# The first three attention tiles in a new order, loads and weight conversions of the start regrouped

## Chip, core and metric

The kernel runs on one core of a Trainium2 chip. The metric is the time of one execution on the device, in microseconds; less is better. TensorE is PE, VectorE DVE, ScalarE ACT, GpSimd POOL, and SyncE (SP) issues most DMAs.

## What is computed

Block attention with a window and block means, a dense block with a gate, and a mixture of eight experts to which tokens are assigned greedily:

```python
scores_l = scale * q @ k^T, kept where |i - j| < 16
scores_s = scale * q @ max over 32 keys(k) + log(32)
a = softmax([scores_l, scores_s])
x = a @ [v, mean over 32 keys(v)]            # 2 batches, 8 heads, 768 x 64
h = x @ w_in                                 # x: 1536 x 512, w_in: 512 x 2048
x = (h * clip(h + 3, 0, 6) / 6) @ w_out
logits = x @ w_gate; each token to one expert, at most 192 tokens an expert
out = relu(x[mask] @ w1[e]) @ w2[e]          # 8 experts, 512 x 1024 and 1024 x 512
```

The weights come to the chip with 64 bits per number, and the kernel makes 32-bit numbers of them.

## The kernel before, in words

The 1536 tokens are 12 tiles of 128 (`NT`), and 4 units of 3 tiles (`UT`, `U` = 384 tokens, `NU` = 4). A tile's attention is done in two halves of four heads. A half (n, h) goes through these steps:

- scores on PE (`front`, L383) into banks 0 and 1, from the queries and from `kw`, the window of keys; DVE adds the mask and takes the minimum (L391, one instruction and a read for each of four pieces);
- exponentials on ACT (`soften`, L402, four pieces), then on DVE two small instructions on the sums (L404, L405; `sm` has two buffers), then one pass of POOL over `A` (L406, "scaling" below);
- transposition on PE (`turn`, L414) and its copy `at` on ACT (L416; two buffers);
- products with the values on PE (`values`, L429) from `VW`, which holds a window of values and the means of all blocks of 32 values; then `emit_x` (from L437): a copy `x` on ACT (L447) and its low half on DVE (L78).

`window` (L368) copies the window of keys for a tile on DVE. `q_prep` (L353, L355) transposes the queries of a tile from the fourth on. The means of the values are a sum on PE in bank 4 (`vsum_mul`, L199, eight products); `vsum_place` copies them on ACT into the three `VW` buffers (L204, three instructions one behind the other).

A slice of `w_in` (16 in all, f0 to f15 below) is loaded by SP into one of four buffers (`w_in_load`, L247), converted by three steps on DVE through bank 3 (L272, "steps" below), then split by `w_split` into `wh` on ACT (L289) and `wl` on POOL (L290). When a slice's third step has been written down, the load of the slice four places on is put on a list (`soon`), which is emitted behind the next piece of work. `gemm1` takes 12 products of PE (L621 to L623) for a slice and unit; ACT adds 3 and takes relu (L624), and DVE's `gate` (L637) sets free the bank, 5 or 6, that the product two slices later needs.

The instructions of each engine run in the order in which the program writes them down. `drive` interleaves several generators by the share of each that is done. Ahead of the first unit, `prologue` (halves of tiles 0 to 2) is interleaved with the first `4 * AHEAD` pieces of `splits` (conversion steps, with a split `CLAG` slices behind). In the first unit `gemm1` is interleaved with the attention of tiles 3 to 5 and the rest of `splits`; `ATTS`, `END`, `S0` and `S1` set how. Somewhere in the first unit SP also issues the loads of the second batch: four for the rows of its keys (L169), two for the sums of its values (L173), and `load_v` (L181) for windows of values. `warm` puts products on PE whose result nobody reads.

Of the kernel before, what the change touches and what calls it, by code (L numbers as in the profile page):

```python
# [42 lines left out]
STEPS = 12  # L43
SEEK, COUNT = 4600, 1900
ROUTE = 100000
CLAG = 2
AHEAD = 6
EARLY = 13
LEFT = 4
VLAG = 0  # L50
VN = 3
ATTS = [31212, 20565, 23910, 18810]
END = [0.92, 0.92, 0.92]
S0 = 0.27
S1 = 0.7
LX = 4
TAIL = [0, 1], [2]

# [30 lines left out]
def build(ctx, tc, q, k, v, w_in, w_out, w_gate, w1, w2, out):  # L89
# [82 lines left out]
    def load_first(x, src, b, hs, rs, r):  # L172
        SP.dma_start(x[:, hs, rs], src[b, hs].rearrange("h (p r) d -> p h r d", r=r)[:x.shape[0], :, rs])  # L173
# [11 lines left out]
    def vsum_load(b, g):  # L185
        load_first(vs, v, b, slice(0, H), RH[g], KR)
# [11 lines left out]
            means.append(bank(4))  # L198
        PE.matmul(means[-1][:KEYS], zones, vs[:, :, i], start=i == 0, stop=last)  # L199

    def vsum_place():
        pv = means[-1][WIN:KEYS, None].rearrange("p a (h d) -> p a h d", d=D).to_broadcast([NB, 2, H, D])
        for x in VW:
            ACT.activation(x[WIN:KEYS], pv, AF.Copy)  # L204

    for g in range(2):
        hs = slice(HP * g, HP * g + HP)
        for rs in RH:
            load_first(k0, k, 0, hs, rs, KR)
        load_first(q0, q, 0, hs, slice(0, UT), UT)  # L210

    for x in VW:
        POOL.memset(x, 0.0)
# [88 lines left out]
    def kprep_first(g):  # L302
        hps = slice(2 * g, 2 * g + 2)
        for i, rs in enumerate(RH):
            for hp in range(2 * g, 2 * g + 2):
                p = bank((2, 3, 5, 6)[2 * i + hp % 2])
                for j in range(4):
                    for z in range(2):
                        PE.matmul(p[64 * z:64 * z + 64, j * KP:(j + 1) * KP], k0[:, 2 * hp + z, 4 * i + j], ident[:KP, :KP],  # L309
                                  start=True, stop=True, skip_group_check=True)  # L310
                ACT.activation(kT[:, hp, rs], p[:, :4 * KP].rearrange("p (r s) -> p r s", r=4), AF.Copy)
                DVE.tensor_reduce((ks if i else kmax)[:, hp], p[:, :4 * KP].rearrange("p (r n s) -> p n r s", r=4, s=4),
                                  axis=AX.XY, op=OP.max)
                yield 450
        DVE.tensor_tensor(ks[:, hps], ks[:, hps], kmax[:, hps], op=OP.max)
# [57 lines left out]
    def front(n, h, after):  # L373
        b, i = divmod(n, 6)
        qT = fr[n] if n else qT0
        A = Abuf[(2 * n + h) % (LAG + 1)]
        sp = [bank(0), bank(1)]
        for pr in range(2):
            hp = 2 * h + pr
            for g in range(2):  # L380
                for s in range(2):
                    r, c = slice(64 * s, 64 * s + 64), slice(QG * g, QG * g + QG)
                    PE.matmul(sp[s][c, pr * KEYS:(pr + 1) * KEYS], qT[r, hp, c], kw[r, hp, g], start=True, stop=True)  # L383
        if after:
            q_prep(n + 1)
        mk = mask[:, 0 if i == 0 else 2 if i == 5 else 1]
        sm = att.tile([128, 3, 4], FT, name="sm", bufs=2)
        for pr in range(2):
            for s in range(2):
                c = 2 * pr + s  # L390
                DVE.tensor_tensor_reduce(out=A[:, c], in0=sp[s][:, pr * KEYS:(pr + 1) * KEYS], in1=mk, scale=-SCALE,  # L391
                                         scalar=3e38, op0=OP.add, op1=OP.min, accum_out=sm[:, 0, c:c + 1])
        if after:
            window(n + 1)
        later.append((A, sm))
# [11 lines left out]

    ats = {}

    def turn(n, h):  # L410
        A = Abuf[(2 * n + h) % (LAG + 1)]
        p = bank(2)
        for c in range(4):
            PE.transpose(p[:KEYS, c * 128:(c + 1) * 128], A[:, c], ident)  # L414
        at = att.tile([128, 4, 128], FT, name="at", bufs=2)
        ACT.activation(at[:KEYS], p[:KEYS].rearrange("p (c s) -> p c s", c=4), AF.Copy)  # L416
        ats[n, h] = at

# [34 lines left out]
    def halves():  # L453
        for n in range(UT, NT):
            b, i = divmod(n, 6)
            if b and i == 0:
                vsum(b)
                yield from kprep(b)
                q_prep(n)
                window(n)  # L460
                yield 2400
            for h in range(2):
                t = pend.pop(0) if len(pend) >= LAG else None
                if t:
                    turn(*t)
                    turned.append(t)
                    yield 660
                after = h == 1 and i < 5
                first = (n, h) == (UT, 1)
                if not first:  # L470
                    front(n, h, after)
                    yield 1250 + 450 * after
                pend.append((n, h))
                while turned:
                    if turned[0] == (6 * b, 0):
                        vsum_mul(0, True)
                        vsum_place()
                    values(*turned.pop(0))
                    yield 1000
                emit_x()  # L480
                if first:
                    yield 1
                    front(n, h, after)
                    yield 1250 + 450 * after
                yield from soften()
                emit_x()
                if (n, h) == (5, 0):
                    for j in range(4):
                        load_rows("kraw", k, 1, j)
                    for g in range(2):  # L490
                        vsum_load(1, g)
            if i == 5:
                while pend or turned:
                    if turned:
                        yield 700
                        values(*turned.pop(0))
                        yield 1000
                        emit_x()
                    if pend:
                        yield 800  # L500
                        t = pend.pop(0)
                        turn(*t)
                        turned.append(t)
                        yield 660
# [269 lines left out]
    def prologue():  # L774
        soft = []

        def half(n, h, after=False):
            front(n, h, after)
            soft.append(soften())
            next(soft[-1])  # L780
            pend.append((n, h))

        def rest():
            for _ in soft.pop(0):
                pass

        def turned_one():
            t = pend.pop(0)
            turn(*t)
            turned.append(t)  # L790

        for c in kprep_first(0):
            yield c
        qprep_first(0)
        window(0, slice(0, 2))
        yield 600
        for c in kprep_first(1):
            yield c
        front(0, 0, False)
        qprep_first(1)  # L800
        warm(6)
        soft.append(soften())
        next(soft[-1])
        pend.append((0, 0))
        yield 1850
        window(0, slice(2, 4))
        half(0, 1, True)
        warm(10)
        rest()
        yield 1250  # L810

        def block_means(i):
            for j in range(i, i + 2):
                vsum_mul(j, j == KR - 1)

        def both(t):
            values(*t)
            emit_x()

        half(1, 0)  # L820
        warm(6)
        rest()
        yield 1250
        turned_one()
        yield 660
        half(1, 1, True)
        warm(6)
        rest()
        yield 1700
        block_means(0)  # L830
        yield 1700
        turned_one()
        yield 660
        block_means(2)
        yield 1700
        half(2, 0)
        rest()
        yield 1250
        block_means(4)
        block_means(6)  # L840
        vsum_place()
        yield 3400
        warm(8)
        both(turned.pop(0))
        yield 1000
        turned_one()
        yield 660
        both(turned.pop(0))
        yield 1000
        half(2, 1, True)  # L850
        rest()
        yield 1700
        both(turned.pop(0))
        yield 1000
        turned_one()
        yield 660
        rest()
        yield from attend_unit(0)

    w_in_load(0)  # L860
    for g in range(2):
        vsum_load(0, g)
    load_v(0)
    w_in_load(1)
    w_in_load(2)
    load_v(1)
    w_in_load(3)
    load_rows("qraw", q, 0, UT)
    load_v(2)
    load_rows("qraw", q, 0, UT + 1)  # L870

    def splits():
# [6 lines left out]
            yield 1  # L879

    splitting, second = splits(), gemm2()
    drive([[prologue(), ATTS[0], 0, 1], [part(splitting, 4 * AHEAD), 4 * AHEAD, S0, 1.0]], soon)
    tlast = late = None
    for u in range(NU):
        st = []
# [427 lines left out]
```

## Time and profile before

| | |
|---|---|
| median of 3 runs | 579.42 us (577.53 to 581.66) |
| the profiled execution | 577.43 us |
| its span on the core | 575.3 us |
| mean granted clock of PE, share of full speed | 0.994 |
| PE busy | 551.1 us (96%) |
| DVE busy | 355.1 us (62%) |
| ACT busy | 295.2 us (51%) |
| POOL busy | 164.9 us (29%) |

The span begins with the first recorded work on the core and ends with the last; the 2.1 us between span and execution lie around it. All starts below count from the span's start. A busy PE does not mean a PE at full rate: the durations of neighbouring products overlap, so the space between the starts of two products is their price. In a row, a bracket behind an instruction gives the idle time of its engine ahead of it and what ended it.

### The profile page before, as it was taken

What the parts mean: (1) busy time and instruction counts of PE and PEld (TensorE: products, weight loads), DVE (VectorE), ACT (ScalarE), POOL (GpSimd) and SP (SyncE); (2) the same over time, 40 slices, a digit from 0 to 9 for tenths busy, and PEclk for the clock granted to TensorE, in tenths of its full rate; (3) what the DMA queues carried; (4) which work ended last, traced back from release to release, by engine and by line L of the source; (5) the groups of instructions that cost most, each with busy time, mean ns of one, the idle gap of its engine ahead of it and who ended that gap; (6) DMA issues with size and microseconds to landing.
All of it is one profiled execution on the core that took longest, in us unless ns stands there. A gap on an engine that the chain in (4) does not pass through costs nothing.

```text
span 575.3 us, 10978 instructions
## 1 busy us (share of the span) xinstructions
PE 551.1 (96%) x3939; PEld 463.2 (81%) x3939; DVE 355.1 (62%) x1020; ACT 295.2 (51%) x702; POOL 164.9 (29%) x198
## 2 busy tenths in 40 slices
PE   6979999999999999999999999999999999999993
PEld 6757889878899989976677777777889988998882
DVE  7778893634543497730055555644687888888870
ACT  4666664556555355651232232325576767676750
POOL 2235467011211033562244444455001110111011
PEclk9999999999999999999999999999999999999998
DMA  9998696122100254420070000014698978998811
GB/s 242 245 224 203 156 228 118 38 47 47 26 2 2 75 183 147 146 66 1 1 206 14 1 1 1 0 51 167 180 273 256 271 228 256 284 265 241 258 33 32
DMA packets 98270, 75.05 MB, mean 130 GB/s; under 512 B 38112, under 2 KB 84704, under 8 KB 98208
## 3 DMA queue, kind: packets, MB, share of 16 engines
q1 hardware_dynamic: 96224, 67.96, 44.0%
q0 software_dynamic: 1984, 6.32, 3.0%
q8 instruction: 33, 0.54, 0.4%
q14 instruction: 29, 0.24, 0.1%
HBM read 67.55 MB, written 6.71 MB: 129 GB/s over the span
## 4 chain that ended last, share of the span: by engine, by line
PE 57%; issue 26%; DVE 5%; POOL 4%; ACT 3%; DMA 3%; SPq 0%; POOLq 0%; DVEq 0%
PE bank L738 8%; PE bank L739 7%; PE bank L740 7%; PE bank L621 7%; PE bank L622 6%; PE bank L623 6%; POOL out_dram L1116 3%; PE bank L383 2%; PE bank L649 2%; PE bank L429 2%; PE bank L199 1%; DMA big<-in_moe_w_out_dram 1%; PE bank L414 1%; PE bank L309 1%; PE bank L573 1%
## 5 line engine op out<-in xcount | busy, mean ns | idle before, releaser
L621 PE MATMUL bank<-x,wh 128*128 128x384 f32 x256 | 91.5, 357 | 2.4 <-DVE t L637 2.2
L299 DVE TENSOR_TENSOR wl<-t,wh 128x1024 fp32r<-128x1024 f32 x64 | 77.0, 1220 | 20.5 <-ACT wh L298 19.9
L622 PE MATMUL bank<-x,wh 128*128 128x384 f32 x256 | 86.0, 336 | 0.4 <-DVE x L78 0.3
L623 PE MATMUL bank<-x,wl 128*128 128x384 f32 x256 | 86.1, 336 | 0.0
L715 ACT ACTIVATE thx<-t 128x384 fp32r<-128x384 f32 (+2 forms) x80 | 36.2, 459 | 94.6 <-PE bank L739 93.7
L624 ACT ACTIVATE t<-bank,three 128x384 f32<-128x384 f32 x64 | 37.1, 580 | 84.8 <-PE bank L623 83.3
L738 PE MATMUL bank<-wh,thx 128*128 128x512 f32 x192 | 79.2, 412 | 0.0
L716 POOL TENSOR_TENSOR tlx<-t,thx 128x384 fp32r<-128x384 f32 (+1 forms) x56 | 56.0, 1002 | 77.1 <-ACT thx L715 70.4
L740 PE MATMUL bank<-wh,tlx 128*128 128x512 f32 x192 | 75.3, 392 | 0.1
L739 PE MATMUL bank<-wl,thx 128*128 128x512 f32 x192 | 75.0, 390 | 0.0
L1141 PE MATMUL bank<-x,wh 128*128 128x384 f32 x256 | 73.7, 360 | 0.5 <-DVE x L1067 0.5
L298 ACT ACTIVATE wh<-t 128x1024 fp32r<-128x1024 f32 x64 | 65.6, 1047 | 0.0
L1143 PE MATMUL bank<-x,wl 128*128 128x192 f32 x256 | 64.2, 251 | 0.0
L637 DVE SCALAR_TENSOR_TENSOR t<-t,bank 128x384 f32<-128x384 f32 x64 | 34.9, 549 | 44.7 <-ACT t L624 44.7
L406 POOL TENSOR_TENSOR A<-A,sm 128x480 f32<-128x480 f32 x24 | 23.7, 987 | 113.5 <-ACT at L416 68.3
L1116 POOL DMA_INDIRECT out_dram<-t,idx x16 | 14.9, 930 | 141.5 <-DVE t L1165 136.0
L621 PEld LDWEIGHTS bank<-x,wh 128*128 128x128 f32 x256 | 48.0, 188 | 6.5 <-DVE t L637 3.6
L1143 PEld LDWEIGHTS bank<-x,wl 128*128 128x128 f32 x256 | 48.9, 191 | 0.3
L1141 PEld LDWEIGHTS bank<-x,wh 128*128 128x128 f32 x256 | 48.1, 188 | 1.2 <-DVE x L1067 0.8
L622 PEld LDWEIGHTS bank<-x,wh 128*128 128x128 f32 x256 | 48.2, 188 | 1.0 <-DVE x L78 0.9
L1157 PE MATMUL bank<-wh,t 128*128 128x512 f32 x128 | 49.0, 391 | 0.0
L623 PEld LDWEIGHTS bank<-x,wl 128*128 128x128 f32 x256 | 48.1, 188 | 0.0
(195 smaller groups left out, 1028.0 us busy)
## 6 DMA issues: line engine op xcount, KB each, us to landing
t<-in_moe_w_dram SPq DMA_DIRECT2D x128, 256.0 KB, 4.6
t<-in_moe_w_in_dram SPq DMA_DIRECT2D x16, 512.0 KB, 5.3
big<-in_moe_w_out_dram SPq DMA_DIRECT2D x16, 512.0 KB, 3.4
VW<-in_v_dram SPq DMA_DIRECT2D x20, 192.0 KB, 4.7
t<-in_v_dram SPq DMA_DIRECT2D x4, 768.0 KB, 12.2
raw<-in_q_dram SPq DMA_DIRECT2D x9, 256.0 KB, 4.1
t<-xs SPq DMA_DIRECT2D x8, 258.0 KB, 3.4
t<-in_k_dram SPq DMA_DIRECT2D x4, 384.0 KB, 5.6
```

The lines of the kernel that those rows point to most:

```text
L298: ACT.activation(hi, x, AF.Copy)
L299: DVE.tensor_tensor(lo, x, hi.bitcast(FT), op=OP.subtract)
L621: PE.matmul(p, wh[:, kk, :], xh[:, kk, :], start=kk == 0, stop=False)
L622: PE.matmul(p, wh[:, kk, :], xl[:, kk, :], start=False, stop=False)
L623: PE.matmul(p, wl[:, kk, :], xh[:, kk, :], start=False, stop=kk == KD - 1)
L716: (DVE if placed[0] else POOL).tensor_tensor(ths[i][1], t, ths[i][0].bitcast(FT), op=OP.subtract)
L738: PE.matmul(acc[j], th[:, c], WH[s], start=f == 0, stop=False)
L739: PE.matmul(acc[j], th[:, c], WL[s], start=False, stop=False)
L740: PE.matmul(acc[j], tl[:, c], WH[s], start=False, stop=f == NF - 1)
L1141: PE.matmul(p, a[:, kk, :], xt[:, kk].rearrange("p c s -> p (c s)"), start=kk == 0, stop=False, skip_group_check=True)
L1143: PE.matmul(p[:, :CAP], b[:, kk, :], xt[:, kk, 0, :], start=False, stop=kk == KD - 1, skip_group_check=True)
L1157: PE.matmul(p, x, w, start=m == 0 and i == 0, stop=m == NM - 1 and i == 2)
```

## The change

Four things are rewritten, all at the start of the program.

- **Loads.** All four loads of the keys of batch 0 stand ahead of the two of its queries. The first half of the values for the means stands ahead of the first slice of `w_in`; the later loads of slices and values are in another order.
- **Prologue.** Two products for the means stand behind the scores of each half from (0, 1) on, where before the eight stood in three places later. `vsum_place` now writes one `VW` buffer, and its three calls stand at three places. One transposition gets a buffer of its own (`early.t`), so that three copies `at` can live. The windows of tiles 1 and 2 are made earlier or later by a half. 10 products of `warm` are left of 36. `prologue` ends behind half (2, 1): the scores and the exponentials of (3, 0) and the rest move into the first unit.
- **Conversions.** The prologue calls the steps itself, and 3 slices (`AHEAD`) instead of 6 are converted ahead of the first unit; a slice is split one slice behind (`CLAG`) instead of two. The other 13 slices are converted in the first unit.
- **Numbers of the planner.** `ATTS`, and one constant `S1` (0.82 instead of 0.7).

```diff
-CLAG = 2
-AHEAD = 6
+CLAG = 1
+AHEAD = 3
...
-ATTS = [31212, 20565, 23910, 18810]
+ATTS = [1, 21817, 26418, 18414]
 END = [0.92, 0.92, 0.92]
-S0 = 0.27
-S1 = 0.7
+S1 = 0.82
...
-    def vsum_place():
+    def vsum_place(i):
         pv = means[-1][WIN:KEYS, None].rearrange("p a (h d) -> p a h d", d=D).to_broadcast([NB, 2, H, D])
-        for x in VW:
-            ACT.activation(x[WIN:KEYS], pv, AF.Copy)
+        ACT.activation(VW[i][WIN:KEYS], pv, AF.Copy)
 
     for g in range(2):
-        hs = slice(HP * g, HP * g + HP)
         for rs in RH:
-            load_first(k0, k, 0, hs, rs, KR)
-        load_first(q0, q, 0, hs, slice(0, UT), UT)
+            load_first(k0, k, 0, slice(HP * g, HP * g + HP), rs, KR)
+    for g in range(2):
+        load_first(q0, q, 0, slice(HP * g, HP * g + HP), slice(0, UT), UT)
...
-    def turn(n, h):
+    def turn(n, h, at=None):
...
-        at = att.tile([128, 4, 128], FT, name="at", bufs=2)
+        if at is None:
+            at = att.tile([128, 4, 128], FT, name="at", bufs=2)
...
+        def conv(n):
+            for _ in range(n):
+                next(splitting)
...
+        half(1, 0)
+        conv(2)
+        rest()
+        turned_one()
+        block_means(2)
+        yield 1
+        half(1, 1)
+        window(2)
+        rest()
+        conv(2)
+        turned_one()
+        block_means(4)
+        yield 1
         half(2, 0)
         rest()
+        conv(2)
         block_means(6)
-        vsum_place()
...
+        vsum_place(0)
+        turned_one(early.t[:, :512].rearrange("p (c s) -> p c s", c=4))
+        yield 1
+        half(2, 1)
+        window(UT)
+        rest()
+        both()
+        vsum_place(1)
+        turned_one()
+        yield 1
+        conv(2)
+        both()
+        yield 1
+        vsum_place(2)
+        rest()
+        conv(2)
+        warm(4)
+        both()
+        turned_one()
+        yield 1
+        q_prep(UT)
+        both()
+        yield 1
+        conv(2)
+        turned_one()
+        both()
+        yield 1
+        both()
+        yield 1
 
-    w_in_load(0)
     for g in range(2):
         vsum_load(0, g)
+        if g == 0:
+            w_in_load(0)
     load_v(0)
     w_in_load(1)
+    load_v(1)
     w_in_load(2)
-    load_v(1)
-    w_in_load(3)
     load_rows("qraw", q, 0, UT)
     load_v(2)
+    w_in_load(3)
...
-    drive([[prologue(), ATTS[0], 0, 1], [part(splitting, 4 * AHEAD), 4 * AHEAD, S0, 1.0]], soon)
+    drive([[prologue(), 1, 0, 1]], soon)
```

On SP's queue, these are the loads that the first unit issues late in it, in before; `t<-in_moe_w_in_dram` is a slice of `w_in`, and the next rows load keys, values and windows of values of the second batch:

```order
L247 DMA t<-in_moe_w_in_dram 128x4x256 x2
L169 DMA t<-in_k_dram 128x8x64 x4
L173 DMA t<-in_v_dram 96x8x256 x2
L181 DMA VW_95<-in_v_dram 96x8x64 x2
L181 DMA VW_96<-in_v_dram 96x8x64 x2
```

And the same place in after:

```order
L245 DMA t<-in_moe_w_in_dram 128x4x256 x3
L168 DMA t<-in_k_dram 128x8x64 x4
L172 DMA t<-in_v_dram 96x8x256 x2
L245 DMA t<-in_moe_w_in_dram 128x4x256
L180 DMA VW_95<-in_v_dram 96x8x64 x2
L180 DMA VW_96<-in_v_dram 96x8x64 x2
```

The last slice's load (f15) now stands behind the six loads of the second batch instead of ahead of them.

On DVE, the end of the conversions in the first unit, before; `bank_1037` and `bank_1070` are bank 3 for the last two slices, f14 and f15, and the L637 rows are the gates of f9 to f12:

```order
L272 SCALAR_TENSOR_TENSOR bank_1037<-t,bank_1037 128x512
L637 SCALAR_TENSOR_TENSOR t<-t,bank_1040 128x384
L272 SCALAR_TENSOR_TENSOR t<-t,bank_1037 128x512
L272 TENSOR_SCALAR bank_1070<-t 128x512
L404 TENSOR_SCALAR sm<-sm 128x4
L405 RECIPROCAL sm<-sm 128x4
L78 TENSOR_TENSOR x<-bank_952,x 128x4x128
L272 SCALAR_TENSOR_TENSOR bank_1070<-t,bank_1070 128x512
L272 SCALAR_TENSOR_TENSOR t<-t,bank_1070 128x512
L637 SCALAR_TENSOR_TENSOR t<-t,bank_1082 128x384
L637 SCALAR_TENSOR_TENSOR t<-t,bank_1113 128x384
L637 SCALAR_TENSOR_TENSOR t<-t,bank_1137 128x384
```

And in after, where `bank_1067` and `bank_1097` are bank 3 for the last two slices, and the L637 rows are the gates of f11, f12 and f13:

```order
L270 TENSOR_SCALAR bank_1067<-t 128x512
L637 SCALAR_TENSOR_TENSOR t<-t,bank_1069 128x384
L270 SCALAR_TENSOR_TENSOR bank_1067<-t,bank_1067 128x512
L270 SCALAR_TENSOR_TENSOR t<-t,bank_1067 128x512
L270 TENSOR_SCALAR bank_1097<-t 128x512
L270 SCALAR_TENSOR_TENSOR bank_1097<-t,bank_1097 128x512
L637 SCALAR_TENSOR_TENSOR t<-t,bank_1099 128x384
L270 SCALAR_TENSOR_TENSOR t<-t,bank_1097 128x512
L637 SCALAR_TENSOR_TENSOR t<-t,bank_1129 128x384
```

The conversions end three gates later, and the first two steps of the last slice stand ahead of the gate of f12.

On ACT, the placing of the means in before (L204), with the copies and exponentials that follow:

```order
L204 ACTIVATE VW_94<-bank_408 24x1024
L204 ACTIVATE VW_95<-bank_408 24x1024
L204 ACTIVATE VW_96<-bank_408 24x1024
L289 ACTIVATE wh<-t 128x512
L416 ACTIVATE at<-bank_484 120x512
L447 ACTIVATE x<-bank_472 128x4x128
L355 ACTIVATE qT<-bank_517 128x512
L402 ACTIVATE A_92,sm<-A_92,sm 128x120 x4
```

And in after:

```order
L202 ACTIVATE VW_94<-bank_326 24x1024
L415 ACTIVATE t<-bank_425 120x512
L400 ACTIVATE A_92,sm<-A_92,sm 128x120 x4
L202 ACTIVATE VW_95<-bank_326 24x1024
L415 ACTIVATE at<-bank_466 120x512
L287 ACTIVATE wh<-t 128x512
L446 ACTIVATE x<-bank_456 128x4x128
L202 ACTIVATE VW_96<-bank_326 24x1024
L415 ACTIVATE at<-bank_510 120x512
L353 ACTIVATE qT<-bank_521 128x512
```

The three are apart, and the last one, which sets bank 4 free for the values of tile 1, stands behind the exponentials of half (2, 1), a split and a copy `x`.

## Rows read from the trace of the kernel before

**Rows 1.** Busy time by stretch: us, engines' busy us (instructions), PEclk, DMA share, GB/s.

```profile
0.00:48.70 48.70, 39.71 (x520) 31.84 (x520) 36.21 (x133) 29.35 (x86) 14.95 (x22) 0.96 1.01 235
48.70:97.00 48.30, 46.52 (x393) 42.15 (x392) 37.56 (x105) 28.57 (x80) 26.77 (x20) 1.00 0.80 179
```

**Rows 2.** Chain that ended last, 28 to 50 us: start, us, what.

```profile
32.45 2.84 ACT VW L204 x3
48.49 0.70 DVE x L78
49.23 0.44 PE bank L622
```

**Rows 3.** Timeline of PE, 33 to 45 us: start, us, instruction, count [idle before].

```profile
34.13 0.69 PE L429 MATMUL bank<-at,VW 120*64 120x64 f32 x16
41.76 0.62 PE L414 MATMUL bank<-ident,A 128*120 128x128 f32 x4 [2.09 <-ACT at L416]
43.32 1.97 PE L429 MATMUL bank<-at,VW 120*64 120x64 f32 x32
```

**Rows 4.** Busy time by stretch, 44 to 45 us, columns as in rows 1.

```profile
44.00:45.00 1.00, 1.00 (x26) 1.00 (x22) 1.00 (x7) 0.51 (x2) 1.00 (x1) 0.50 0.97 332
```

**Rows 5.** Timeline of POOL and DVE, 19.5 to 20.8 us.

```profile
19.55 0.99 POOL L406 TENSOR_TENSOR A<-A,sm 128x480 f32<-128x480 f32 x1 [15.17 <-DVE sm L405]
20.57 0.28 DVE L391 CUSTOM_DVE_ANT_0 A<-bank,mask 128x120 f32<-128x120 f32 x1 [1.17 <-POOL A L406]
```

**Rows 6.** Timeline of ACT, 29 to 41.5 us.

```profile
29.27 0.40 ACT L402 ACTIVATE A<-A,sm 128x120 f32<-128x120 f32 x1 [2.14 <-DVE sm L391]
...
40.52 0.62 ACT L289 ACTIVATE wh<-t 128x512 fp32r<-128x512 f32 x1
41.04 0.58 ACT L416 ACTIVATE at<-bank 120x512 f32<-120x512 f32 x1
```

**Rows 7.** Timeline of DVE, 69 to 74 us.

```profile
69.47 0.55 DVE L637 SCALAR_TENSOR_TENSOR t<-t,bank 128x384 f32<-128x384 f32 x1
69.94 0.69 DVE L272 TENSOR_SCALAR bank<-t 128x512 int32<-128x512 int32 x1
...
72.80 0.28 DVE L391 CUSTOM_DVE_ANT_0 A<-bank,mask 128x120 f32<-128x120 f32 x1
...
73.61 0.55 DVE L637 SCALAR_TENSOR_TENSOR t<-t,bank 128x384 f32<-128x384 f32 x1
```

**Rows 8.** DVE groups, 49 to 85.6 us: count | busy, mean ns | idle.

```profile
L368 DVE COPY kw<-kT 128x384 f32<-128x384 f32 (+1 forms) x4 | 3.1, 792 | 0.0
L405 DVE RECIPROCAL sm<-sm 128x4 f32<-128x4 f32 x5 | 0.9, 178 | 0.2
L404 DVE TENSOR_SCALAR sm<-sm 128x4 f32<-128x4 f32 x5 | 0.8, 164 | 1.0 <-ACT A L402 1.0
```

**Rows 9.** Timeline of DVE, 41.8 us: such an instruction beside a POOL pass.

```profile
41.79 0.73 DVE L404 TENSOR_SCALAR sm<-sm 128x4 f32<-128x4 f32 x1
```

**Rows 10.** Timeline of SP's DMA queue, 73 to 93 us.

```profile
73.34 4.75 SPq L169 DMA_DIRECT2D t<-in_k_dram  x4
...
80.24 12.28 SPq L181 DMA_DIRECT2D VW<-in_v_dram  x4
```

**Rows 11.** DMA issued at 72.5, 80.2, 92 us: KB each, us to landing.

```profile
t<-in_moe_w_in_dram SPq DMA_DIRECT2D x1, 512.0 KB, 4.4
VW<-in_v_dram SPq DMA_DIRECT2D x1, 192.0 KB, 11.3
VW<-in_v_dram SPq DMA_DIRECT2D x1, 192.0 KB, 3.4
```

**Rows 12.** Timeline of PE at the last slices of the first unit.

```profile
86.17 0.45 PE L621 MATMUL bank<-x,wh 128*128 128x384 f32 x1 [0.66 <-DVE t L637]
...
88.39 0.60 PE L414 MATMUL bank<-ident,A 128*120 128x128 f32 x4
...
96.37 1.04 PE L334 MATMUL bank<-ident,t 128*128 128x128 f32 x8
```

More of the change, by code (lines that the diff above doesn't have):

```diff
@@ L476, in halves @@
                         vsum_mul(0, True)
-                        vsum_place()
+                        for j in range(3):
+                            vsum_place(j)
                     values(*turned.pop(0))
@@ L775, in prologue, with half @@
         soft = []
-        def half(n, h, after=False):
-            front(n, h, after)
+        def half(n, h):
+            front(n, h, False)
             soft.append(soften())
@@ L785, in rest, with turned_one @@
                 pass
-        def turned_one():
+        def turned_one(at=None):
             t = pend.pop(0)
-            turn(*t)
+            turn(*t, at)
             turned.append(t)
[L792 to L810, printed above, removed]
         def block_means(i):
@@ L814, in block_means, with both @@
                 vsum_mul(j, j == KR - 1)
-        def both(t):
-            values(*t)
+        def both():
+            values(*turned.pop(0))
             emit_x()
+        def conv(n):
+            for _ in range(n):
+                next(splitting)
+        for c in kprep_first(0):
+            yield c
+        window(0, slice(0, 2))
+        for c in kprep_first(1):
+            yield c
+        window(0, slice(2, 4))
+        qprep_first(0)
+        qprep_first(1)
+        yield 1
+        half(0, 0)
@@ L820, in prologue @@
+        warm(6)
+        yield 1
+        half(0, 1)
+        window(1)
+        rest()
+        block_means(0)
+        yield 1
         half(1, 0)
-        warm(6)
+        conv(2)
         rest()
-        yield 1250
         turned_one()
-        yield 660
-        half(1, 1, True)
-        warm(6)
+        block_means(2)
+        yield 1
+        half(1, 1)
+        window(2)
         rest()
-        yield 1700
-        block_means(0)
-        yield 1700
+        conv(2)
         turned_one()
-        yield 660
@@ L834, in prologue @@
-        block_means(2)
-        yield 1700
+        block_means(4)
+        yield 1
         half(2, 0)
         rest()
-        yield 1250
-        block_means(4)
+        conv(2)
         block_means(6)
[L841 to L845, printed above, removed]
-        turned_one()
[L847 to L850, printed above, removed]
+        vsum_place(0)
+        turned_one(early.t[:, :512].rearrange("p (c s) -> p c s", c=4))
@@ L851, in prologue @@
+        yield 1
[4 more added lines that the diff above has]
+        vsum_place(1)
+        turned_one()
+        yield 1
[3 more added lines that the diff above has]
+        vsum_place(2)
         rest()
-        yield 1700
-        both(turned.pop(0))
-        yield 1000
+        conv(2)
+        warm(4)
+        both()
         turned_one()
-        yield 660
-        rest()
-        yield from attend_unit(0)
-    w_in_load(0)
+        yield 1
+        q_prep(UT)
@@ L861, in build @@
+        both()
+        yield 1
+        conv(2)
+        turned_one()
+        both()
+        yield 1
+        both()
+        yield 1
     for g in range(2):
         vsum_load(0, g)
+        if g == 0:
+            w_in_load(0)
     load_v(0)
     w_in_load(1)
+    load_v(1)
     w_in_load(2)
-    load_v(1)
-    w_in_load(3)
     load_rows("qraw", q, 0, UT)
     load_v(2)
+    w_in_load(3)
     load_rows("qraw", q, 0, UT + 1)
```

## The prediction, made before the changed kernel was run

> **What bounds the kernel now.** I read the table of stretches first: which engine is full, and where. Ahead of the first unit PE is busy 39.7 of 48.7 us, and part of that is filler; in the first unit 46.5 of 48.3, with DVE at 37.6, its highest share in the program [rows 1]. The rest of the span, behind 97 us, is the same code in nearly the same order, and I take it as unchanged, ±1 us. So two stages count: what ends the wait for the first unit, and whether PE or DVE then sets its pace.
>
> The chain of waits says what ended the first stage: three placings of the means on ACT, 32.45 to 35.29, and at its end the low half of tile 2's `x`, for which PE's first L622 waited until 49.23 [rows 2]. Two more views matter. On PE's timeline an idle time of 2.1 us ends at 41.76, and soon after 32 products take 1.97 us where 16 took 0.69 before [rows 3]; the stretch 44 to 45 us has a granted clock of 0.50 [rows 4], the 1.2 GHz level. So here a wait of about 2 us was followed by half clock. In the first unit PE waits for a gate of DVE, 0.66 us ahead of 86.17 [rows 12]; its last slice ends at 96.37, where key transpositions begin [rows 12].
>
> **The change, part by part.**
>
> *Start of the first unit.* DVE may write the scores' sums of a half only when POOL has scaled the half two before it, since `sm` has two buffers: a POOL pass from 19.55 takes 0.99, and DVE starts at 20.57, released by it [rows 5]. Two conversion steps of 0.69 [rows 7] now stand ahead of one such scaling: half (1, 1) comes 1.4 to 1.5 later. But ahead of the scores of (2, 0) there is one step now instead of five, 4 x 0.69 = 2.8 less. The exponentials of (2, 0) so begin about 1.1 earlier than 29.27 [rows 6], at 28.2. From there ACT's row has no gap: exponentials 1.5 (four pieces at 0.39), a placing 0.95 (2.84 / 3 [rows 2]), a copy 0.55, exponentials 1.5, placing 0.95, copy 0.55, split 0.5 (40.52 to 41.04 [rows 6]), `x` 0.5, third placing 0.95: 7.9, so 36.1. PE has its other work done by about 33.4 and waits 2.7 us there, because bank 4 is wanted for the values of tile 1. Then the chain has values 0.7, a transposition 0.6 [rows 3], its copy 0.6, `qT` 0.5, `x` 0.5, split 0.5, copy 0.6, values 0.7, `x` 0.6, low half 0.7 [rows 2]: 6.0, at 42.1. A wait of 2.7 us is longer than the 2.1 that preceded half clock, so I add 1.0 for about half of that PE work at half rate (1.97 against 2 x 0.69 is +0.6 for each 32 products). L622 begins at **43.0**, 6.2 earlier than 49.23. Without a fall of the clock 41.5; with more of it 45.
>
> *What moves into the unit.* Three slices (9 steps, 6.2 us), scores and scaling of (3, 0), its window of tile 4 and two splits: some 8.5 us more for a DVE that had 10.7 us left [rows 1]. DVE becomes the pace until its conversions are done. From the first gate (f0 takes 2.2, as 86.17 to 88.39 [rows 12], relu 0.6, so 45.8) to the third step of slice 10 its order has 23 steps x 0.69 = 15.9; 8 gates x 0.47 (69.47 to 69.94 [rows 7]) = 3.8; 4 sets of scores x 0.81 (72.80 to 73.61 [rows 7]) = 3.2; 4 scalings x 0.34 [rows 8] = 1.4; 4 copies of windows x 0.79 [rows 8] = 3.2; a low half 0.7: 28.2. Idle ahead of scalings was 1.0 for five [rows 8]: +0.8. Slice 10 is done at T = **74.8** (between 73 and 77).
>
> Is a scaling's first instruction really 0.16? Alone beside a POOL pass it once took 0.73 [rows 9]; the mean of five in the unit is 0.164 [rows 8], and I take that; the other end would be +2.3 for four. The Trainium skill, "SBUF — State Buffer", section "SBUF: two separate sides", says that some DVE instructions and GpSimd's take a shared port as an exclusive lock; by it more DVE work beside more POOL work would stretch both, some 2 us in T as an estimate. The 0.164 speaks against that here, the 0.73 for it.
>
> *The load of the last slice.* Before, the loads of slices 14 and 15 both went out ahead of the second batch's keys, the last at about 73. Now slice 14's is released at T, then SP issues four loads of keys and two for the means, and only then slice 15's: from 73.34 the keys took 4.75, and the first `VW` load came at 80.24 [rows 10], 7.4 after the slice's own issue at 72.8. So slice 15's is issued at T + 7.4 = 82.2. What was issued at that place landed 11.3 us later; with an empty queue it was 3.4, and a lone slice took 4.4 [rows 11]. I take 11.3, since the same six loads stand ahead: landing at **93.5**. The bounds: 4.4 gives 86.6, and a slice has 512 KB where the `VW` load had 192, so 13 would give 95.2. The Trainium skill, "DMA: Bandwidth & Descriptors", section "Queues, rings and completion order", says that descriptors are taken in ring order on each DMA engine, and this agrees with 11.3 behind six loads and 3.4 behind none; it also says that completion is not first in, first out, and no run here shows that for a slice behind the keys.
>
> DVE wants the slice after 12 more steps (8.3), 4 gates (1.9), scores 0.8, two scalings 0.7 and a low half 0.7: T + 12.4 = 87.2. It waits 6.3 us. Behind that step stands the gate of f12, and PE's f14 waits for that gate's bank, so PE stops too.
>
> *The end of the unit.* From landing: two steps and the gate 1.9, f14 2.2, transpositions 0.5, f15 2.2, and about 0.9 because PE idles some 6 us, three times the wait that preceded half clock: 7.7, end at 101.2, against 96.37: **+4.8**. The start's gain of 6.2 is in this sum already: it is eaten by 6.2 us of steps and by the wait for one load.
>
> *At nothing.* The removed filler products end where PE waits anyway; if the clock needed them, that is the third case below. Keys ahead of queries: both halves of both are wanted before the first scores, and the last byte is the same one. The first slice of `w_in` later: its first step stands behind the scores of (1, 0), after 20.57 [rows 5]. Products of the means between scores: the same eight. If any of these is wrong it moves the first exponentials by at most 1 us, either way, and T with it.
>
> *Sum.* 577.43 + 4.8 = 582.2 on the profiled execution, which lies 2.0 under the median of 579.42; so 584.2 against the median, 582.2 if that execution is the fairer start. I forecast **583.0**. Its own range goes by T from 73 to 77 and the landing from 11.3 - 2 to 13: 579 to 587.
>
> **Rivals.**
>
> *The slice lands in time.* If the keys' loads do not hold it up, it lands before 87.2, as a lone slice's 4.4 us would (86.6) [rows 11]. Then DVE runs through, PE loses nothing but DVE's pace, and the unit ends at 87.2 + 1.9 + 2.2 + 0.5 + 2.2 = 94.0: -2.4, so 575.0 by the profiled execution and **577** by the median; with the start at 41.5 it is 575.5. For it: 4.4. Against it: 11.3 at this very place. Chance 0.22.
>
> *Slower: half clock lasts into the unit.* The wait of 2.7 us at bank 4, and no filler behind it, puts the values, transpositions and f0 on the 1.2 GHz level. f0 then costs 2.2 more and the pieces before it 2 instead of 1: the first gate comes 3.2 later, and since DVE is full from there on, everything behind shifts by it, the late load too: **586.5**, 1.2% over the median. It decides from 2.2 us over my sum (585.2 is 1%). For it: 0.50 after a shorter wait [rows 4]. Against: that half clock was over before the unit, whose stretch shows 1.00 [rows 1]. Chance 0.20.
>
> *The order changes little.* If DVE has more slack than I count, the start's gain and the load's wait cancel: 579. Chance 0.05.
>
> **How the numbers follow.** Forecast 0.53. A measurement of this kernel can tell about 1% (5.8 us) from no change: 573.6 and 585.2. Of the forecast's 0.53 some 0.12 lie over 585.2; of the slower rival's 0.20 some 0.15; with 0.01 from elsewhere slower is 0.28. Faster by 1% needs the slice in time and the earliest start together, 0.12. The rest, 0.60, is within 1%. The range for 8 in 10 reaches from 574.0 (the slice in time, and a start near 42) to 589.0 (half clock and a landing after 13 us).
>
> **What would show it.** In the profile after: PE's first L622 near 43, with an idle time of 2 to 3 us ahead of the values of tile 1 that ends with ACT's L202; DVE without gaps from 46 to 87, then an idle time of about 6 us that ends with a DMA of `w_in`; on PE an idle time of the same size ahead of f14, ended by the gate; the granted clock at 0.5 behind one or both; the last product of the unit near 101. I am wrong if the slice lands less than 6 us after its issue (then about 577), if L622 begins after 45 (then over 585), or if the part behind the first unit differs by more than 1.

## The result, and the profile after

The changed kernel takes 587.77 us (median of 4 runs, 587.02 to 589.67), the kernel before 579.16 (4 runs, 577.53 to 581.66): a ratio of 1.015, with a 95% interval of 1.0105 to 1.0194. That is slower by 1.5%, inside the range and 4.8 us over the forecast.

The two profiled executions are not alike at their start. The exponentials of half (0, 1), an early place at which the two programs have done the same work, begin here:

```profile
17.64 0.40 ACT L402 ACTIVATE A<-A,sm 128x120 f32<-128x120 f32 x1 [0.30 <-DVE sm L391]
```

in before, and in after:

```profile
19.53 0.40 ACT L400 ACTIVATE A<-A,sm 128x120 f32<-128x120 f32 x1 [0.48 <-DVE sm L389]
```

That is 1.9 us later, and a run below, after with the first half as in before, begins there at 19.11 too, so the change is not the reason. So I count from this place in every execution and call it the anchor. The profiled execution of after (589.67) is the longest of its four, the one of before (577.43) lies under all four of its own; the 12.2 us between them are 8.6 between the medians.

PE's timeline in after, the rows that answer to [rows 2, 3, 12]:

```profile
38.24 0.87 PE L428 MATMUL bank<-t,VW 120*64 120x64 f32 x16 [2.79 <-ACT VW L202]
...
45.87 0.44 PE L622 MATMUL bank<-x,wh 128*128 128x384 f32 x1 [0.28 <-DVE x L77]
...
59.03 0.69 PE L623 MATMUL bank<-x,wl 128*128 128x384 f32 x1 [2.29 <-POOL wl L288]
...
101.59 0.69 PE L621 MATMUL bank<-x,wh 128*128 128x384 f32 x1 [4.40 <-DVE t L637]
...
105.60 1.06 PE L332 MATMUL bank<-ident,t 128*128 128x128 f32 x4
...
108.75 1.03 PE L332 MATMUL bank<-ident,t 128*128 128x128 f32 x8
```

The reader sees four things. The wait for bank 4 stands where it was forecast (2.79, ended by the third placing). Half clock follows there: the granted clock is 0.50, the 1.2 GHz level, from 39 to 42 us, and 1.00 in the next. A stretch of after, columns as in [rows 1]:

```profile
41.00:42.00 1.00, 1.00 (x18) 0.88 (x17) 0.00 (x0) 0.60 (x1) 0.00 (x0) 0.50 0.00 0
```

L622 comes 26.3 us after the anchor; before it was 49.23 - 17.64 = 31.6, so the start gained 5.3. In the unit there is a wait for POOL that I had not seen coming (2.29). And ahead of f14 PE stands for 4.4 us behind a gate; f14 then takes 4.0 us (101.59 to 105.60) where a slice took 2.2 [rows 12]. From L622 to the last transpositions it is 62.9 us, where before it was 47.1: 15.7 lost against 5.3 gained.

What DVE and SP did at that place, DVE's timeline first, then SP's queue, which answers to [rows 10]:

```profile
93.44 0.69 DVE L270 SCALAR_TENSOR_TENSOR t<-t,bank 128x512 int32<-128x512 int32 x1
99.66 0.69 DVE L270 TENSOR_SCALAR bank<-t 128x512 int32<-128x512 int32 x1 [5.53 <-DMA t<-in_moe_w_in_dram]
```

```profile
80.73 5.04 SPq L168 DMA_DIRECT2D t<-in_k_dram  x4
85.82 1.95 SPq L172 DMA_DIRECT2D t<-in_v_dram  x2
87.88 0.67 SPq L245 DMA_DIRECT2D t<-in_moe_w_in_dram  x1
```

The last slice is issued 7.2 us behind the first load of keys and is there 11.8 us later; DVE has waited 5.5 us for it. The waits of PE from L622 to the unit's end, in sum, number and longest:

```profile
PE bank L623 <- POOL wl L288: 5.4, 5, 2.3
PE bank L621 <- DVE t L637: 4.4, 1, 4.4
```

In before, the waits for gates in the first unit were 1.4 us, and none was for `wl`:

```profile
PE bank L621 <- DVE t L637: 1.4, 2, 0.8
```

Stretches of after around the late load, with columns as in [rows 1]:

```profile
97.00:103.00 6.00, 1.60 (x12) 1.46 (x7) 2.44 (x4) 0.83 (x2) 0.12 (x1) 0.75 1.07 148
103.00:110.00 7.00, 7.00 (x36) 6.87 (x36) 2.74 (x5) 2.87 (x7) 6.92 (x3) 0.72 0.16 37
```

DMA is full (1.07) while the engines stand for most of the time (PE is busy 1.6 of 6 us, DVE 2.4), and then PE works at a mean clock of 0.72 to 0.75, part of it at the 1.2 GHz level. Behind the first unit both programs are alike: from the transpositions to the span's end it is 478.9 us in both (575.3 - 96.37 and 587.6 - 108.75). In the profiled executions of the runs below the same part takes 478.4 to 481.2, so a unit that ends 2 us earlier need not show in a single time.

### The profile page after: what moved, and what is told of

It reads as the page before. It is cut to its first block, busy times and chain, and to the rows that moved or that the text cites. A ratio compares the mean times of both kernels' runs of the same rounds, so it can differ in the third digit from the quotient of the medians.

```text
span 587.6 us, 10874 instructions
## 1 busy us (share of the span) xinstructions
PE 551.9 (94%) x3887; PEld 461.5 (79%) x3887; DVE 355.3 (60%) x1020; ACT 296.9 (51%) x702; POOL 164.9 (28%) x198
## 4 chain that ended last, share of the span: by engine, by line
PE 51%; issue 27%; POOL 9%; ACT 5%; DVE 4%; DMA 2%; POOLq 0%; SPq 0%; DVEq 0%
PE bank L738 7%; PE bank L621 6%; PE bank L740 6%; PE bank L739 6%; PE bank L623 6%; PE bank L622 6%; POOL out_dram L1125 3%; POOL xs L671 2%; PE bank L649 2%; PE bank L428 2%; ACT A L400 2%; POOL A L404 2%; PE bank L307 1%; PE bank L381 1%; POOL wl L288 1%
## 5 line engine op out<-in xcount | busy, mean ns | idle before, releaser
L621 PE MATMUL bank<-x,wh 128*128 128x384 f32 x256 | 92.9, 363 | 5.4 <-DVE t L637 5.3
L623 PE MATMUL bank<-x,wl 128*128 128x384 f32 x256 | 88.2, 344 | 5.4 <-POOL wl L288 5.4
L622 PE MATMUL bank<-x,wh 128*128 128x384 f32 x256 | 87.2, 341 | 0.3 <-DVE x L77 0.3
L1150 PE MATMUL bank<-x,wh 128*128 128x384 f32 x256 | 73.7, 360 | 0.5 <-DVE x L1076 0.5
L637 DVE SCALAR_TENSOR_TENSOR t<-t,bank 128x384 f32<-128x384 f32 x64 | 35.0, 550 | 40.7 <-ACT t L624 40.7
L621 PEld LDWEIGHTS bank<-x,wh 128*128 128x128 f32 x256 | 49.2, 192 | 8.9 <-DVE t L637 6.0
L622 PEld LDWEIGHTS bank<-x,wh 128*128 128x128 f32 x256 | 49.4, 193 | 0.5 <-DVE x L77 0.5
L1150 PEld LDWEIGHTS bank<-x,wh 128*128 128x128 f32 x256 | 48.0, 188 | 1.2 <-DVE x L1076 0.8
```

Of the source, the lines that this page charges most:

```text
L621: PE.matmul(p, wh[:, kk, :], xh[:, kk, :], start=kk == 0, stop=False)
L622: PE.matmul(p, wh[:, kk, :], xl[:, kk, :], start=False, stop=False)
L623: PE.matmul(p, wl[:, kk, :], xh[:, kk, :], start=False, stop=kk == KD - 1)
L1150: PE.matmul(p, a[:, kk, :], xt[:, kk].rearrange("p c s -> p (c s)"), start=kk == 0, stop=False, skip_group_check=True)
```

## Experiments

Three theories were open. A: the late load of the last slice is what makes the kernel slower. B: DVE and POOL are too full in the unit, whatever the load does. C: the wait for bank 4 takes a part of the start's gain away. All ratios are to the kernel before, run beside them on the same chip. No run takes back the prologue's new order as a whole, `ATTS`, `S1` or `CLAG` by themselves, so what share of the start's 5.3 us each of them has is not shown.

**The last slice's load first.** The six loads of the second batch are taken out of the attention's code and put on the list behind the slice's load:

```diff
...
         if s + NW < NF:
             soon.append(partial(w_in_load, s + NW))
+            if s + NW == NF - 1:
+                soon.append(second_batch)
...
```

> After, but the six loads of the second batch are issued behind the last slice's load instead of ahead of it; nothing else moves. Theory A (the late load sets the end of the first unit): the DVE wait of 5.5 us ahead of the last slice's first step and the PE wait of 4.4 us ahead of f14 go, f14 runs at full clock (2.2 instead of 4.0 us), so the first unit ends some 6 to 7 us earlier than 108.75 and the time is about 581. Rival B (DVE and POOL are full in the unit, and the wait for the load only hides that): the unit ends at most 2 us earlier, about 586.

Measured: 583.25 us, 1.0043 (1.0026 to 1.006). DVE's wait for the load and PE's for the gate of f12 are gone. PE's timeline at the end, then the waits that are left:

```profile
98.96 0.60 PE L340 MATMUL bank<-ident,t 128*128 128x128 f32 x4
...
101.49 1.04 PE L340 MATMUL bank<-ident,t 128*128 128x128 f32 x8
```

```profile
PE bank L626 <- POOL wl L296: 5.4, 5, 2.3
PE bank L420 <- POOL A L412: 0.8, 1, 0.8
```

The unit ends 82.3 us after the anchor instead of 89.2: 6.9 less, and the ratio falls by 1.1%, some 6 us. A holds for the larger part. But the kernel is still 0.43% over before, and the waits for `wl` are what they were (5.4): a loss in the unit itself, as B has it, is left.

**The late load alone, in the kernel before.** The same edit the other way round: the six loads go on the list ahead of the slice's.

```diff
...
         if s + NW < NF:
+            if s + NW == NF - 1:
+                soon.append(second_batch)
             soon.append(partial(w_in_load, s + NW))
...
```

> Before, with one edit: the six loads of the second batch are issued ahead of the last slice's load, as in after. Theory A: issued at about 77 and landing 11 us later at about 88, where DVE wants it at about 76; DVE waits some 10 us, the gate of f10 behind it stops PE at f12, and the unit ends 8 us later, 587 (585 to 590). Rival B: with six slices converted ahead of the unit the wait is hidden by what PE has in hand, 579 to 581.

Measured: 590.74 us, 1.0183 (1.0155 to 1.021), which is 10.6 us by the ratio and 9.7 by the medians (581.04 beside it) for this one edit: more than the 8 I expected, and the time lies over the 585 to 590. In the trace the unit is 8.3 longer (55.4 from L622 to its end, where it was 47.1). DVE's timeline, then PE's:

```profile
90.42 0.69 DVE L278 TENSOR_SCALAR bank<-t 128x512 int32<-128x512 int32 x1 [6.20 <-DMA t<-in_moe_w_in_dram]
```

```profile
93.89 0.69 PE L624 MATMUL bank<-x,wh 128*128 128x384 f32 x1 [6.84 <-DVE t L640]
```

The wait is shorter than the 10 us I expected (other work of DVE stands ahead of that step), yet PE's wait behind it is 6.8, and 1.2 GHz follows (0.50 in the stretches at 92, 94 and 96 us). Six slices in hand do not hide it. So the order on one queue costs alone about as much as the whole change does with all its gains (1.0183 against 1.015; the intervals overlap).

**The three placings together.**

```diff
-        vsum_place(0)
+        for j in range(3):
+            vsum_place(j)
         turned_one(early.t[:, :512].rearrange("p (c s) -> p c s", c=4))
...
-        vsum_place(1)
         turned_one()
...
-        vsum_place(2)
         rest()
```

> After, but with the three placings of the means one behind the other where the first one stands, as in before. Theory C (the third placing, which holds bank 4, costs the start its wait of 2.8 us and the half clock behind it): no such wait, granted clock 1.0 from 38 to 42 us, first L622 at 42.5 to 43.5 instead of 45.87, time about 585. Rival: the exponentials of half (2, 1) come 2 us later and end the same chain, L622 not before 45.3, time about 587.5.

Measured: 587.53 us, 1.0117 (1.0092 to 1.0142). PE's timeline:

```profile
34.28 1.06 PE L412 MATMUL bank<-ident,A 128*120 128x128 f32 x4 [1.85 <-ACT t L415]
...
44.20 0.44 PE L622 MATMUL bank<-x,wh 128*128 128x384 f32 x1 [0.28 <-DVE x L77]
```

The wait for bank 4 is gone, but 1.85 us of waiting stand earlier, now for a copy that ACT does behind the three placings, and 1.2 GHz follows there. L622 is 25.4 after the anchor (18.83), 1.0 less than in after and between what the theory and the rival expected. C names the right place, but two thirds of the wait only move. The ratio is 0.33% lower, within the intervals' overlap.

**Filler in the wait for bank 4.**

```diff
-        warm(4)
+        warm(26)
```

> After, with 26 filler products instead of 4 ahead of the values of tile 1, which is 2.8 us more of them in the wait of 2.8 us for bank 4. Theory C split in two: if the half clock behind the wait costs what the rows say (3.4 us at half), the granted clock stays 1.0 and the first L622 comes at about 44.4 instead of 45.87, time about 586.4. Rival: filler only takes the place of the wait and the chain on ACT sets the start, L622 within 0.4 us of 45.87 and no change.

Measured: 588.12 us, 1.0147 (1.0111 to 1.0183). My size was wrong: a call makes two products (so the 10 and 36 of `warm` in the change are calls too).

```profile
33.66 6.07 PE L152 MATMUL bank<-ident 128*128 128x128 f32 x52
39.67 0.69 PE L428 MATMUL bank<-t,VW 120*64 120x64 f32 x16
```

The filler ran 2.1 us past the third placing, which ended at 37.57. The clock stayed at 1.0, and the one took back what the other gave (L622 26.9 after the anchor). So it was run again:

```diff
-        warm(4)
+        warm(15)
```

> After, with 15 filler calls (two products each) instead of 4 ahead of the values of tile 1: the 26 of the run before were 6.07 us and ran 2.1 us past the end of the third placing. Theory (the half clock behind the wait costs the start 1.5 to 2 us): granted clock 1.0 from 38 to 42 us, first L622 at 43.8 to 44.4, time 1.5 to 2 us under after. Rival (the chain on ACT sets the start, PE's clock is hidden): L622 within 0.4 of 45.8, no change.

Measured: 586.63 us, 1.014 (1.0113 to 1.0167).

```profile
33.12 3.62 PE L152 MATMUL bank<-ident 128*128 128x128 f32 x30
37.08 0.69 PE L428 MATMUL bank<-t,VW 120*64 120x64 f32 x16 [0.34 <-ACT VW L202]
...
43.21 0.44 PE L622 MATMUL bank<-x,wh 128*128 128x384 f32 x1 [0.28 <-DVE x L77]
```

The values of tile 1 begin 18.7 after the anchor (18.38), as in after (38.24 - 19.53), and L622 is 24.8 after it, 1.5 less than in after, with a clock of 1.0 between them: this is what half clock cost the start. Of the time it is at most visible: 1.5 us are 0.26%, about the width of the interval to either side, so the median does not show whether they reach the end. Nor do the traces: the unit ends 84.8 after the anchor here and 85.6 in the run with 26 calls, against 89.2 in after, which is far more than L622 moved. In these two DVE waited 3.5 and 3.7 for the slice instead of 5.5. Both are the shortest executions of their four, and the medians do not bear 4 us out.

**More slices ahead of the unit.** On top of the run with the slice's load first, one slice more is converted in the prologue, where DVE had nothing to do:

```diff
-AHEAD = 3
+AHEAD = 4
...
-        conv(2)
+        conv(6)
         turned_one()
         both()
```

> After with the last slice's load ahead of the second batch's, and one slice more (four) converted ahead of the first unit, its three steps in the stretch 38.4 to 42.7 us in which DVE has nothing to do. Theory B in its second form (what is left over before comes from conversions that POOL and DVE finish late in the unit: PE waits 5.4 us for wl): those waits fall under 2.5 us, no half clock at 59 us, the unit ends 3 to 4 us earlier than the 101.5 of the run with the load alone, time within 0.2% of before. Rival (the waits come from the order in which POOL takes scalings and splits, whatever is ahead): the waits stay over 4 us, ratio to before 1.004.

Measured: 578.12 us, 0.9981 (0.9963 to 0.9999). The waits of PE, and the end of the unit:

```profile
PE bank L626 <- POOL wl L296: 2.3, 3, 1.2
```

```profile
97.69 1.04 PE L340 MATMUL bank<-ident,t 128*128 128x128 f32 x8
```

The longest wait, for f3, is gone with the half clock behind it; the waits for `wl` are 2.3 in sum instead of 5.4. The unit ends 78.5 after the anchor (19.23), 3.9 less than with the load alone. So the rest of the loss goes when the fourth slice is not left to the unit. That DVE and POOL were too full, as B has it, is more than this shows; the part on the prediction comes back to it.

**All of it.** The three placings together and 8 filler calls in their wait, with four slices ahead:

```diff
-        vsum_place(0)
+        for j in range(3):
+            vsum_place(j)
...
         both()
-        vsum_place(1)
+        warm(8)
         turned_one()
...
-        vsum_place(2)
         rest()
         conv(2)
-        warm(4)
```

> As the run with four slices ahead and the load moved, with the three placings together and 8 filler calls in the wait of 1.85 us that this order had at 32.4 (the 4 of after are taken out). If the single readings add up, L622 at 42 to 43, the unit ends 3 us earlier than with four slices ahead alone, and the time is 0.2 to 0.6% under before. If the gain at the start is given back in the unit (DVE or POOL as its pace), the time is that of the run with four slices ahead.

Measured: 576.62 us, 0.9942 (0.9919 to 0.9966), under before by 0.6%. L622 is 24.8 after the anchor (43.55 - 18.80), 2.1 less than with four slices ahead alone (46.13 - 19.23), but the unit's end, 77.7, is only 0.8 less, where 3 had been expected: most of the gain at the start is given back in the unit, which begins at half clock (0.50 from 44 to 47 us). With five slices ahead (`conv(10)`):

> As the run before this one, with five slices ahead: three more steps on DVE ahead of the low halves that open the unit. If the fifth slice's steps find DVE free, 1 us less than with four; if the slice has not landed, or its steps push the low half of tile 2, L622 comes 1 to 3 us later and the time is that much longer.

Measured: 575.17 us, 0.9941 (0.9918 to 0.9964), and once more, later on the same chip:

> The kernel with five slices ahead once more, as the base of the run before this one on the same chip: 0.994 of before (0.992 to 0.997) by both theories.

577.34 us, 0.9943 (0.9931 to 0.9955). The waits of PE in the first of the two:

```profile
PE bank L626 <- POOL wl L296: 0.6, 1, 0.6
PE bank L625 <- DVE x L77: 0.4, 1, 0.4
```

The waits for `wl` are down to 0.6 in sum, the unit is 49.8 us from L622 to its end (43.80 to 93.56), but the fifth slice's steps put the first low halves back, as L622 comes 25.4 to 25.8 after the anchor instead of 24.8. So neither the 1 us less nor a longer time came: four and five slices can't be told apart by time, and both beat before.

**The first half as before.** Keys and queries loaded in turn, and the scores of half (0, 0) ahead of the second transpositions of queries, in the kernel with five slices ahead and, alone, in after:

```diff
     for g in range(2):
         for rs in RH:
             load_first(k0, k, 0, slice(HP * g, HP * g + HP), rs, KR)
-    for g in range(2):
         load_first(q0, q, 0, slice(HP * g, HP * g + HP), slice(0, UT), UT)
...
         for c in kprep_first(0):
             yield c
+        qprep_first(0)
         window(0, slice(0, 2))
         for c in kprep_first(1):
             yield c
-        window(0, slice(2, 4))
-        qprep_first(0)
+        front(0, 0, False)
         qprep_first(1)
...
+        window(0, slice(2, 4))
         half(0, 1)
```

> The run with five slices ahead, with the first half's way of before: keys and queries loaded in turn, and the scores of half (0, 0) ahead of the transpositions of the second half of the queries. In after the first exponentials began at 17.42, in before at 15.75. If this delay of 1.7 us runs through the whole start (the scaling of each half releases the half two behind it), the first exponentials come at 15.8, L622 1.2 to 1.7 us earlier than with five slices ahead, and the time is 1 to 1.5 us less, 0.7 to 0.85% under before. If the delay is taken up by waits later in the start, the ratio stays 0.994.

> After, with only the loads of keys and queries and the first half in the order of before. If the delay of 1.7 us of the first exponentials runs through, the first exponentials come at 15.8 and L622 at 44.2 to 44.7 instead of 45.87; the late slice's load still ends the unit, but its trigger moves along, so the time is 1 to 1.7 us under after, ratio to before about 1.012. If it is taken up by the wait for bank 4, L622 stays at 45.9 and the ratio at 1.015.

Measured: 0.9934 (0.9921 to 0.9947) beside 0.9943 on the same chip, and 1.0141 (1.0122 to 1.0159). ACT's timeline in the second:

```profile
17.22 0.36 ACT L399 ACTIVATE A<-A,sm 128x120 f32<-128x120 f32 x1
...
19.11 0.39 ACT L399 ACTIVATE A<-A,sm 128x120 f32<-128x120 f32 x1 [0.30 <-DVE sm L388]
```

The expectation rested on a comparison between two executions, 17.42 against 15.75, and it falls: with the order of before the first exponentials begin at 17.22 here, and those of (0, 1) at 19.11, in after at 19.53. The 1.9 us between the profiled executions are a later start of that execution and no effect of the edit. With five slices ahead the same exponentials begin at 18.82 with the old order and at 18.76 with the new one. This part of the change costs and gains nothing that can be measured.

## Why the prediction was right or wrong

It was right in its order of events: gain at the start, the slice's load behind six others, DVE and then PE standing for it. It was right that the sum is a loss, and too low in its size. Its likeliest case lay within 1% of before, and the result is over it; the case "slower by over 1%" had 0.28. The result also lies just over the forecast's own 579 to 587. That the range for 8 in 10 holds it is luck: its upper end, 589.0, was kept for half clock that lasts into the unit and a landing after 13 us, and neither happened. The sign "L622 begins after 45 (then over 585)" came by the clock (45.87) and not by the anchor (26.3 + 17.64 = 43.9), and the time is over 585 for other reasons. The sign "DVE without gaps from 46 to 87" did not come. Term by term, in the profiled executions:

| step | predicted | measured | |
|---|---|---|---|
| start: first L622 after the anchor | 25.4 (43.0 - 17.64) | 26.3 | +0.9 |
| L622 to the first load of keys (T) | 31.8 | 34.9 (80.73 - 45.87) | +3.1 |
| from there to the slice's landing | 18.7 | 18.9 (99.66 - 80.73) | +0.2 |
| landing to the unit's end | 7.7 | 9.1 (108.75 - 99.66) | +1.4 |
| the execution's own later start | 0 | 1.9 | +1.9 |

The sum is 7.5, which is 108.75 against the 101.2 forecast. Without the last line, which is none of the change, 5.6 are left.

**T was the step that failed.** It took DVE as the pace, with 0.8 us of waiting. DVE's timeline in after:

```profile
51.65 2.27 DVE L366 COPY kw<-kT 128x384 f32<-128x384 f32 x2
...
63.25 0.55 DVE L637 SCALAR_TENSOR_TENSOR t<-t,bank 128x384 f32<-128x384 f32 x1 [2.75 <-ACT t L624]
```

From the first gate (48.71) to T DVE stood for 3.9 us: 2.75 ahead of this gate, the rest ahead of scores and a scaling. Where 0.8 had been counted, this is the 3.1 of the table. (The wait of 1.48 ahead of the first gate was in the forecast.) DVE waited because PE itself was behind: it waited for `wl` of f3, and then had half clock. The run with 26 filler calls has the same wait of 2.29 without half clock behind it, and its T is 33.3 after L622 (79.07 - 45.80), by this row of its SP queue:

```profile
79.07 4.41 SPq L168 DMA_DIRECT2D t<-in_k_dram  x4
```

So about half of the 3.1 is the wait, the other half the clock. I had counted the moved slices' steps on DVE, but not that their splits on ACT and POOL come just as late, and that PE then needs them at once. POOL's timeline there:

```profile
56.76 0.99 POOL L404 TENSOR_TENSOR A<-A,sm 128x480 f32<-128x480 f32 x1 [3.21 <-DVE sm L403]
57.71 2.51 POOL L288 TENSOR_TENSOR wl<-t,wh 128x512 fp32r<-128x512 f32 x2
```

POOL was not full: it stood for 3.21 us, while the `wh` that this `wl` takes off was done at 54.5 (ACT's L287 at 53.84, 0.62 long). The scaling stands ahead of the split in POOL's order, and it waited for the sums, which DVE made behind two window copies and a slice's steps. By these rows it is this order, with DVE as its pace, that made PE wait. A run with the split ahead of the scaling was not made, so this is argued and not shown. The run with four slices ahead, where f3 is converted before the unit, takes the wait and the half clock behind it away, and with them the rest of the loss.

**The tail** was short by 1.4: I put 0.9 on the clock, and f14 alone took 1.8 more than a slice at full clock.

**The start** held: the wait of 2.7 us at bank 4 was 2.79, half clock followed, and the price of 1.0 for it measured 1.5 in the run with filler.

**The load** held best: 11.3 us to landing against 11.8, and DVE's wait 6.3 against 5.5. The rival that the slice lands in time is ruled out; as an experiment it is the run with the load first, which kept 6 us. Its price was wrong as well: 577 had the unit at DVE's pace with nothing lost in waits, and that run stayed 0.43% over before. The Trainium skill, "DMA: Bandwidth & Descriptors", section "Queues, rings and completion order", has descriptors taken in ring order on each DMA engine; the traces agree: with the slice behind the six loads it is 11.8 us from issue to DVE's first step in after (87.88 to 99.66) and 10.5 in the kernel before with the loads swapped (79.97 to 90.42), and with the slice ahead of them DVE has no wait for it.

**The rival that half clock lasts into the unit** was right in its time (586.5) and not in its mechanism: half clock was over before the unit began, and came back in it behind other waits.

**At nothing** held for the keys ahead of the queries, which measure nothing in two kernels. The removed filler has its price through the clock at bank 4, the 1.5 above, which the prediction had as 1.0 in the start. The other two were not tried alone. The first instruction of a scaling took 0.167 us in the mean of four from the first gate to T, as taken.

## What to carry to other kernels

When work moves from one stage to a fuller one, count it on every engine that the moved piece goes through, and look for the consumer with the least in hand: here the three slices were counted on DVE, and the 3.1 us that the sum lacked came from their splits on POOL and from PE, which wanted them at once. When a release moves later on a queue that runs in order, list what has passed it: one load of 512 KB behind six others cost some 10 us in a kernel that was otherwise as before. And before two profiled executions are compared by their clocks, find a place where both have done the same, and count from there.

## What was not expected of the hardware

A wait of the same length is not always followed by half clock. PE waited 2.29 us for `wl` of f3 in after and in the run with 26 filler calls:

```profile
58.94 0.44 PE L623 MATMUL bank<-x,wl 128*128 128x384 f32 x1 [2.29 <-POOL wl L288]
```

This row is of the run with the filler; its products run on at a clock of 1.0. In after products of 0.52 follow (granted clock 0.50 from 60 to 62 us). The same stretch in after, then in the run with the filler:

```profile
60.00:61.00 1.00, 1.00 (x5) 1.00 (x4) 0.50 (x1) 0.00 (x0) 0.22 (x1) 0.50 0.15 16
60.00:61.00 1.00, 1.00 (x10) 0.75 (x10) 0.41 (x1) 0.02 (x1) 0.14 (x1) 1.00 0.12 40
```

The kernel with five slices ahead, run twice, had a clock of 1.0 throughout its first unit in one profile and 0.50 from 45 to 47 us in the other, behind the same wait of 1.54. What decides it is open.

Two copies of a window took 2.27 us at 51.65, with POOL passes from 51.06 to 53.55 beside them, and 0.96 at 20.02 with POOL idle. The Trainium skill, "SBUF — State Buffer", section "SBUF: two separate sides", has GpSimd and some instructions of DVE hold a shared port one at a time, and this row agrees with it. Over the unit it cancelled out: four copies took 3.3 us where 3.2 were counted, since in before, too, one of the four lay beside a POOL pass and took 1.50 (64.87).

The anchor comes up to 1.5 us apart between executions with the same work ahead of it (18.02 to 19.53 with the start of after, 17.64 to 19.11 with that of before): the first transpositions of keys take 7.35 to 8.5 us in different executions of kernels with the same start. That is as much as several of the effects measured here.
